# Output projection and attention of the row pairs as one written-out sequence for five queues

## The chip, the core and the metric

The kernel runs on one core of a Trainium2 chip. The metric is the device time of one execution in microseconds. The engines are TensorE (PE, with its weight loads as PEld), VectorE (DVE), ScalarE (ACT), GpSimd (POOL) and SyncE (SP), which here issues all DMAs.

## What is computed

For x of 2048 rows and 1024 columns, all in fp32:

```
xn = layernorm(x)
q, k, v = heads(xn @ wqkv)                  # 32 heads of 32
phi(p)  = concat(softmax(p @ w_phi), softmax(-p @ w_phi))     # per head, 64 features
o       = phi(q) (phi(k)^T v) / (phi(q) (phi(k)^T 1) + 1e-6)
s       = concat_heads(o) @ wo
g       = silu((sigmoid(xn @ w_gate) * (xn @ w_up)) @ w_down)
out     = x + s * g
```

## The kernel before

Every large product is done in the same way. An fp32 operand is split into a high part (an ACT copy that rounds) and a low part (a DVE subtraction), and one product is three matmuls (`mm3`, lines 134 to 136: high by high, high by low, low by high). The 2 by 2 block product is done with seven products of sums of blocks instead of eight, named B11, T2, T3, B21, T1, T4 and B22; the sums are made on POOL.

The stages run one after the other: layernorm with the q, k and v projections, the gated unit (`glu`), the down product with its silu gate g, which goes to DRAM as `g_d`, and last, from 2180 us on, the output projection. Features of q, scaled by their denominators, lie in DRAM as `e_d`.

The output projection takes the rows in eight pairs of 128-row tiles (`NTP` = 8, loop variable `tp_`). For each pair there are two kinds of work:

- **Attention of the next pair** (`attend(tp_ + 1)`, twelve entries). `phi_transpose` turns features with four PE transposes into one of two banks (`tpr`) and splits them with ACT and DVE; the feature tiles are two (`whole(47)` and `whole(48)`, one for each row tile u), each holds one half hb of the heads, and `e_load(u)` refills it when both of its parts q have been turned. `numerator` does eight matmuls of 256 columns into two banks (`nmr`), whose halves are copied (ACT, L684) and added (DVE, L685) into two raw tiles (`oraw`). `o_operands` then makes the seven operands from the raw tiles: one POOL subtraction after the first half (L697), three after the second (L700, L701, L705), in place on the raw tiles, and seven splits.
- **Output of this pair**: seven products with four steps each, 84 matmuls of 512 columns (tiles `x`, `w` or `fa`, `fb` by operand), evacuated by DVE (L1215, L1217, L1224, L1227) and ACT (L1213); for the four finished blocks a multiplication by g and an addition of x on POOL (L1228, L1229; for two blocks of the last pair on DVE), a store (L1230) and `gx_load` (L1191 g, L1192 x), which refills two of four half tiles (`gx`, slots 53 and 54).

In the profile all of `whole(47)` and up are `fc`. The emission of the pair's loop interleaves the two kinds by a count: after each step of a product it takes entries of the next pair's attention while two thirds of the steps are ahead of the entries. A scheduler that works with estimated times then places the instructions on each engine's queue within what the dependencies allow. At the start of the kernel another part is emitted from a list of names (`FIRST`) under `in_order`, which makes each engine's instructions of that part keep the order of emission; `queued` holds the last instruction of each engine.

Of the kernel before, what the change touches and what calls it, by code (L numbers as in the profile page):

```python
# [18 lines left out]
P = 128  # L19
# [14 lines left out]
class Ring:  # L34
# [3 lines left out]
    def next(self):  # L38
        self.n += 1
        return self.items[(self.n - 1) % len(self.items)]  # L40
# [9 lines left out]
def hedgehog_glu_kernel(  # L50
# [65 lines left out]
    def halves(*ids):  # L116
        return [slots[i][:, a] for i in ids for a in range(2)]
# [6 lines left out]
    def pair(i):  # L124
        return slots[i][:, 0], slots[i][:, 1]

    def split(o, src):

        nc.scalar.copy(o[0], src)  # L129
        return nc.vector.tensor_sub(o[1], src, o[0].bitcast(F32))  # L130
# [512 lines left out]
    gx = Ring(halves(54, 53))  # L643
# [7 lines left out]
    def e_load(u):  # L651
        tp_, hb = divmod(e_next[u], 2)
        if tp_ < NTP:
            nc.sync.dma_start(whole(47 + u), e_d[2 * tp_ + u, hb])
        e_next[u] += 1

    def phi_transpose(tp_, u, hb, q):
        ps = tpr.next()
        e = whole(47 + u)
        for j in range(4):  # L660
            k = 4 * q + j
            nc.tensor.transpose(ps[:, j * P:(j + 1) * P], e[:, k * P:(k + 1) * P], ident)  # L662
        if u == 0:
            b = run(phu.next(), 2).rearrange("p a b n -> p (a b n)")
            units_ph[hb, q] = b.rearrange("p (a k t) -> p a k t", a=2, t=256)
        ph, cs = units_ph[hb, q], slice(u * P, (u + 1) * P)
        split((ph[:, 0, :, cs], ph[:, 1, :, cs]), ps.rearrange("p (k t) -> p k t", t=P))
        if q:
            e_load(u)

    def numerator(tp_, hb, q):

        ph = units_ph[hb, q]
        kg = slots[KVB[hb]][:, q].rearrange("p (k m) -> p k m", m=P)
        for b in range(2):
            ps = nmr.next()
            for j in range(2):
                k = 2 * j + b
                for a in range(2):
                    nc.tensor.matmul(ps[:, j * 256:(j + 1) * 256], kg[:, k], ph[:, a, k], start=a == 0, stop=a == 1)  # L680
            hi, lo = [slice(r * 64, r * 64 + 64) for r in (b, 1 - b)]
            o = oraw[hb][hi].rearrange("p u (g t) -> p g u t", t=P)[:, 2 * q:2 * q + 2]
            y, z = [ps[r].rearrange("p (j u t) -> p j u t", j=2, u=2) for r in (hi, lo)]
            nc.scalar.copy(o, z)  # L684
            nc.vector.tensor_add(o, o, y)  # L685
        if q:
            o_operands(tp_, hb)

    def o_operand(tp_, i, b):
        split(pair(of[tp_][i]), b)  # L690

    def o_operands(tp_, hb):
        (b11, b12), (b21, b22) = [(o[:, 0], o[:, 1]) for o in oraw]
        if hb == 0:
            of[tp_] = {i: ofr.next() for i in range(7)}
            o_operand(tp_, B11, b11)
            nc.gpsimd.tensor_sub(b11, b12, b11)  # L697
            return
        o_operand(tp_, B22, b22)
        nc.gpsimd.tensor_sub(b12, b22, b12)  # L700
        nc.gpsimd.tensor_sub(b22, b22, b11)  # L701
        o_operand(tp_, T2, b22)
        o_operand(tp_, T3, b12)
        o_operand(tp_, B21, b21)
        nc.gpsimd.tensor_sub(b21, b21, b22)  # L705
        o_operand(tp_, T1, b11)
        o_operand(tp_, T4, b21)

    def attend(tp_):

        out = []
        for hb in range(2):
            tr = {(u, q): (phi_transpose, tp_, u, hb, q) for u in range(2) for q in range(2)}
            nm = [(numerator, tp_, hb, q) for q in range(2)]

            out += [tr[0, 0], tr[0, 1], tr[1, 0], nm[0], tr[1, 1], nm[1]]
        return out
# [407 lines left out]
    for n, (i, j, cs) in enumerate(dsteps):  # L1125
        w, hs = dready[n]
        for c in cs:
            for u in range(4):
                p = 4 * c + u
                mm3(banks[p], cut(pair(hs[c]), slice(u * P, (u + 1) * P)), pair(w),  # L1130
                    j == 0 and i in (B11, T2, T3, T1), j == NJ - 1, skip_group_check=True)
        wfree.append(w)
        hfree.extend(hs.values())
        if n >= ND - 2 * NJ - 8 and len(WO[B21]) < 4 and hfree:
            WO[B21].append(hfree.popleft())
        if n == 20:
            for hb, s in enumerate(KVB):
                nc.sync.dma_start(slots[s].bitcast(F32).rearrange("p a n -> p (a n)"), kvbd_d[hb])
        while down_prep():
            pass  # L1140
        if j == NJ - 1:
            for c in cs:
                for u in range(4):
                    evacuate(i, 4 * c + u)
        if n and n * 32 // 78 > (n - 1) * 32 // 78 and late:
            t, hb = late.pop(0)
            if t == 0:
                nc.sync.dma_start(zb, zb_d[hb])
            with tc.issue_after(last_split[0]):
                q_task(t, hb)  # L1150
        if 40 <= n < 56 and n % 2 == 0:
            wo_prep(*divmod((n - 40) // 2, 4))
        if n == ND - 2 * NJ:
            assert not late and len(WO[B21]) == 4
            block("x1", 4, 4, F32R)
            for i in (T3, B21):
                side.extend([lambda i=i, k=k: wo_prep(i, k) for k in range(4)])
            side.extend([lambda u=u: e_load(u) for u in range(2)])
        if n == ND - NJ:
            step(1000)  # L1160
            side.extend([lambda fn=fn, a=a: fn(*a) for fn, *a in attend(0)])
# [15 lines left out]

    done = (B21, T1, T4, B22)
    result = [(tp_, i) for tp_ in range(NTP) for i in done]
    gxs = {}  # L1180
# [5 lines left out]
    def gx_load():  # L1186
        if result:
            tp_, i = result.pop(0)
            t, cols = rows(tp_, i)
            g, xt = gxs[tp_, i] = gx.next(), gx.next()  # L1190
            nc.sync.dma_start(g, g_d[t, :, cols])  # L1191
            nc.sync.dma_start(xt, x[t * P:(t + 1) * P, cols])  # L1192

    for _ in range(2):
        gx_load()
    abank = {}
    for tp_ in range(NTP):
        nxt = attend(tp_ + 1) if tp_ + 1 < NTP else []
        n = 0
        u1, u2, y11, y21 = [res.next() for _ in range(4)]  # L1200
        for i in range(7):
            if i in opening:
                abank[i] = amm.next()
            ps = abank[{B21: B11, T4: T3, B22: T1}.get(i, i)]
            o = [h.rearrange("p (k t) -> p k t", t=P) for h in pair(of[tp_][i])]
# [6 lines left out]
            if i == B11:  # L1212
                nc.scalar.copy(u1, ps)  # L1213
            elif i == T2:
                nc.vector.tensor_add(u1, u1, ps)  # L1215
            elif i == T3:
                nc.vector.tensor_add(u2, u1, ps)  # L1217
            else:
                g, xt = gxs.pop((tp_, i))
                t, cols = rows(tp_, i)  # L1220
                eng = nc.vector if tp_ == NTP - 1 and i in (T4, B22) else nc.gpsimd
                if i == B21:
                    y = y11
                    nc.vector.tensor_mul(y, g, ps)  # L1224
                else:
                    y = {T1: u2, T4: y21, B22: u1}[i]
                    nc.vector.tensor_add(y, u2 if i == T1 else u1, ps)  # L1227
                    eng.tensor_mul(y, y, g)  # L1228
                eng.tensor_add(y, y, xt)  # L1229
                nc.sync.dma_start(out[t * P:(t + 1) * P, cols], y)  # L1230
                gx_load()


# [27 lines left out]
```

## Time and profile before

| | |
|---|---|
| median of 3 runs | 2411.07 us (2410.2 to 2412.16) |
| profiled execution | 2411.83 us, span 2410.0 us |
| granted PE clock, mean | 0.997 |
| PE busy, share of the span | 99% |
| DVE, ACT, POOL | 73%, 43%, 40% |
| output projection, first matmul to the end | 2180.51 us to 2410.0 us |

The profile is of one execution; its times are microseconds from the span's start. Matmuls overlap each other, so PE counts as busy even where it only runs at the pace of what feeds it; the distance from one matmul's start to the next tells more. A row of the timeline shows the start, the duration, the engine, the line and the tiles; in brackets stands the idle time before it and what ended it.

### The profile page before, as it was taken

To read this page: it belongs to the slowest core of one execution; us is meant where nothing else is said; L and a number is where in the kernel's file an instruction comes from. 1 tells how busy PE (TensorE), PEld (TensorE's weight loads), DVE (VectorE), ACT (ScalarE), POOL (GpSimd) and SP (SyncE) were. 2 spreads that over 40 slices of the span, in tenths; PEclk is the share of its full clock that TensorE was granted. 3 is DMA by queue.
4 is the path that set the end of the run, shared out by engine and by line. 5 is a ranking of instruction groups with operands and counts; after the bars stand their busy time and mean duration, and the time that the engine had idled before them with its cause. 6 is when DMAs were issued, how large, how long until landed. Compare 5 with 4: busy or idle time off the path is not lost.

```text
span 2410.0 us, 31953 instructions
## 1 busy us (share of the span) xinstructions
PE 2376.2 (99%) x11008; PEld 1974.3 (82%) x11008; DVE 1757.3 (73%) x2323; ACT 1029.4 (43%) x1536; POOL 955.6 (40%) x611
## 2 busy tenths in 40 slices
PE   9999999999999999999999999999999999999998
PEld 8888888888888877888888888888888888878776
DVE  8635777767676688658858888646889988866776
ACT  7334344454544434324434444423443334454443
POOL 1332456656565423122434131323333335414554
PEclk9999999999999999999999999999999999999999
DMA  7688977777676777786877666686666666867554
GB/s 256 243 298 301 367 274 256 271 261 271 250 275 237 260 274 253 247 284 219 280 262 260 210 229 210 210 278 231 218 238 232 225 214 226 283 238 253 183 184 137
DMA packets 232292, 596.31 MB, mean 247 GB/s; under 512 B 30528, under 2 KB 30528, under 8 KB 227520
## 3 DMA queue, kind: packets, MB, share of 16 engines
q1 hardware_dynamic: 232128, 594.25, 70.9%
q8 instruction: 87, 1.43, 0.2%
q14 instruction: 77, 0.63, 0.1%
HBM read 359.01 MB, written 235.14 MB: 247 GB/s over the span
## 4 chain that ended last, share of the span: by engine, by line
PE 83%; DVE 7%; DMA 6%; ACT 2%; issue 2%; POOL 0%; SPq 0%; ACTq 0%; DVEq 0%; POOLq 0%
PE bank L134 27%; PE bank L135 26%; PE bank L136 26%; DVE w L130 2%; PE bank L484 1%; PE bank L283 1%; DMA fc<-qkv_d 1%; PE bank L680 1%; PE bank L662 1%; DMA fc<-xo_d 1%; DMA x<-w_phi 1%; DVE p L130 1%; DVE x L130 1%; ACT w L129 0%; DMA x<-x 0%
## 5 line engine op out<-in xcount | busy, mean ns | idle before, releaser
L134 PE MATMUL bank<-x,w 128*128 128x512 f32 x2352 | 912.1, 390 | 5.9 <-ACT x L129 2.9
L135 PE MATMUL bank<-x,w 128*128 128x512 f32 x2352 | 916.4, 390 | 0.0
L136 PE MATMUL bank<-x,w 128*128 128x512 f32 x2352 | 908.0, 390 | 0.0
L129 ACT CAST w<-fa 128x512 fp32r<-128x512 f32 (+1 forms) x430 | 293.4, 686 | 554.6 <-PE bank L135 367.4
L134 PEld LDWEIGHTS bank<-x,w 128*128 128x128 f32 x2352 | 442.0, 188 | 99.8 <-ACT fb L1039 3.5
L136 PEld LDWEIGHTS bank<-x,w 128*128 128x128 f32 x2352 | 442.1, 188 | 91.9 <-DVE w L130 0.4
L135 PEld LDWEIGHTS bank<-x,w 128*128 128x128 f32 x2352 | 442.2, 188 | 90.1
L130 DVE TENSOR_TENSOR w<-fa,w 128x512 fp32r<-128x512 f32 (+1 forms) x430 | 418.7, 978 | 109.1 <-ACT w L129 101.3
L134 PE MATMUL bank<-w,x 128*128 128x512 f32 x708 | 278.7, 394 | 2.2 <-DVE fc L414 2.2
L136 PE MATMUL bank<-w,x 128*128 128x512 f32 x708 | 277.6, 392 | 2.7 <-DVE x L829 2.7
L135 PE MATMUL bank<-w,x 128*128 128x512 f32 x708 | 276.9, 391 | 0.0
L1049 POOL TENSOR_TENSOR fb<-fb,fc 128x512 f32<-128x512 f32 x57 | 88.1, 1546 | 244.5 <-DVE fc L1048 241.7
L136 PEld LDWEIGHTS bank<-w,x 128*128 128x128 f32 x708 | 133.3, 188 | 32.3 <-DVE x L829 3.8
L134 PEld LDWEIGHTS bank<-w,x 128*128 128x128 f32 x708 | 133.5, 189 | 30.0 <-DVE fc L414 2.5
L135 PEld LDWEIGHTS bank<-w,x 128*128 128x128 f32 x708 | 133.4, 188 | 26.4
L619 POOL TENSOR_TENSOR fc<-fc 128x1024 f32<-128x1024 f32 x32 | 81.5, 2546 | 183.1 <-ACT fc L449 127.5
L1048 DVE TENSOR_TENSOR fc<-fc,bank 128x512 f32<-128x512 f32 x84 | 57.2, 681 | 106.4 <-PE bank L136 98.0
L130 DVE TENSOR_TENSOR x<-fa,x 128x512 fp32r<-128x512 f32 x112 | 112.2, 1002 | 18.7 <-ACT x L129 18.5
L129 ACT CAST w<-fb 128x512 fp32r<-128x512 f32 x112 | 69.3, 619 | 129.1 <-PE bank L135 94.1
L129 ACT CAST p<-fc 128x1024 fp32r<-128x1024 f32 (+2 forms) x97 | 70.8, 735 | 109.8 <-DVE fc L465 63.9
L130 DVE TENSOR_TENSOR p<-fc,p 128x1024 fp32r<-128x1024 f32 (+2 forms) x97 | 105.3, 1094 | 16.0 <-ACT p L129 13.8
L130 DVE TENSOR_TENSOR w<-fb,w 128x512 fp32r<-128x512 f32 x112 | 94.5, 845 | 30.1 <-ACT w L129 25.0
(256 smaller groups left out, 3197.6 us busy)
## 6 DMA issues: line engine op xcount, KB each, us to landing
ws_d<-w SPq DMA_DIRECT2D x112, 512.0 KB, 4.2
w<-ws_d SPq DMA_DIRECT2D x112, 512.0 KB, 4.9
fa<-w_gu SPq DMA_DIRECT2D x84, 512.0 KB, 3.8
fa<-h_d SPq DMA_DIRECT2D x84, 512.0 KB, 4.1
fa<-wf_d SPq DMA_DIRECT2D x32, 1024.0 KB, 7.1
h_d<-fc SPq DMA_DIRECT2D x120, 256.0 KB, 3.3
fc<-e_d SPq DMA_DIRECT2D x48, 512.0 KB, 3.9
fc<-qkv_d SPq DMA_DIRECT2D x80, 256.0 KB, 4.6
```

Of the source, the lines that this page charges most:

```text
L129: nc.scalar.copy(o[0], src)
L130: return nc.vector.tensor_sub(o[1], src, o[0].bitcast(F32))
L134: nc.tensor.matmul(o, a[0], b[0], start=first, stop=False, **kw)
L135: nc.tensor.matmul(o, a[0], b[1], start=False, stop=False, **kw)
L136: nc.tensor.matmul(o, a[1], b[0], start=False, stop=last, **kw)
L283: nc.tensor.matmul(ps[:, gs], r[:, gs], bd[:, 4 * f + g], start=True, stop=True)
L484: nc.tensor.matmul(kvb[g // 2][:, g % 2 * 256:g % 2 * 256 + 256], v[:, g].rearrange("p a f -> p (a f)"), ph[:, g].rearrange("p a f -> p (a ...
L619: nc.gpsimd.tensor_mul(ez, e, zb)
L662: nc.tensor.transpose(ps[:, j * P:(j + 1) * P], e[:, k * P:(k + 1) * P], ident)
L680: nc.tensor.matmul(ps[:, j * 256:(j + 1) * 256], kg[:, k], ph[:, a, k], start=a == 0, stop=a == 1)
L1048: v = nc.vector.tensor_add(b, u2 if q == 3 else u1, bank)
L1049: nc.gpsimd.tensor_mul(g, g, b)
```

## The change

The loop over pairs is replaced by a list of names, `PAIR`, emitted for each of the first seven pairs, and a list `LAST` for the eighth. Everything is emitted under `in_order` for PE, DVE, ACT, POOL and SP, so all five queues keep the order of the list. The functions of attention are cut into single parts: `tr` u hb q (four transposes), `hi` and `lo` (the splits), `nm` hb q b (four matmuls), `cp` and `ad` (their evacuation), `s11`, `sA`, `sB`, `sC` (the POOL subtractions), `x`..`h` and `x`..`l` (the operand splits). `g`..k is one step of a product, `v` its evacuation, `m` and `a` the multiplication by g and the addition of x, `y` the store, `l` the loads of g and x for two results later, `e` u hb a feature load. Attention parts in the list belong to pair `tp_ + 1`. The order of the products within a pair is B11, T2, B21, T3, T1, T4, B22.

For the last pair, the multiplication and addition of block B22 are arranged otherwise: POOL computes u1 * g + x ahead (`rest`), and after the last product DVE multiplies the bank by g and adds the two. The loads of g and x for the last two results go into the feature tiles, which are free by then. `attend` without an argument serves the first pair only, as before; in it a feature load is now emitted ahead of the split of the features that it replaces.

As built, each queue holds the same work as before (on DVE one instruction fewer, on POOL two more), and in the steady pairs the SP queue holds four times (load of g, load of x, store), then four feature loads in a row, where it held feature loads between the others before.

```diff
-    for _ in range(2):
-        gx_load()
-    abank = {}
-    for tp_ in range(NTP):
-        nxt = attend(tp_ + 1) if tp_ + 1 < NTP else []
-        n = 0
...
-            for k in range(4):
-                mm3(ps, (o[0][:, k], o[1][:, k]), pair(WO[i][k]), i in opening and k == 0, k == 3, skip_group_check=True)
-                n += 1
-                while nxt and (13 - len(nxt)) * 3 <= 2 * n:
-                    fn, *a = nxt.pop(0)
-                    fn(*a)
...
-                    nc.vector.tensor_add(y, u2 if i == T1 else u1, ps)
-                    eng.tensor_mul(y, y, g)
-                eng.tensor_add(y, y, xt)
-                nc.sync.dma_start(out[t * P:(t + 1) * P, cols], y)
-                gx_load()
+    def gx_load(n):
+        if n < len(result) and result[n] not in gxs:
+            t, cols = rows(*result[n])
+            late = len(result) - 1 - n
+            g, xt = gxs[result[n]] = halves(47 + late) if late < 2 else [gx[(2 * n + a) % 4] for a in range(2)]
+            nc.sync.dma_start(g, g_d[t, :, cols])
+            nc.sync.dma_start(xt, x[t * P:(t + 1) * P, cols])
...
+    PAIR = """
+        gB110 gB111 gB112 tr100 tr000 hi100 gB113 gT20 vB11 gT21 hi000 gT22 lo100 gT23 lo000 gB210 tr001 tr101 e00
+        hi001 nm000 e10 hi101 lo001 gB211 cp000 lo101 gB212 ad000 nm011 vT2 nm001 cp011 gB213 cp001 ad011 gT30 ad001
+        gT31 gT32 gT33 tr010 vT3 tr111 hi010 nm010 hi111 lo010 gT10 cp010 lo111 tr110 ad010 gT11 e11 hi110 xB11h
+        tr011 lo110 gT12 e01 hi011 xB11l nm101 lo011 s11 gT13 cp101 nm100 ad101 gT40 cp100 vB21 xT1h nm111 ad100
+        aB21 gT41 cp111 vT1 nm110 ad111 gT42 cp110 gT43 ad110 gB220 vT4 sA xB22h lB21 gB221 xB21h xB22l yB21 gB222
+        xT3h xB21l sB gB223 vB22 sC xT2h xT3l xT2l mT1 xT4h xT1l aT1 xT4l mT4 lT1 aT4 yT1 lT4 yT4 mB22 aB22 lB22
+        yB22""".split()
+
+    LAST = ("gB110 gB111 gB112 gB113 vB11 gT20 gT21 gT22 gT23 vT2 gB210 gB211 gB212 gB213 vB21 gT30 gT31 gT32 gT33 aB21 vT3 "
+            "yB21 gT10 gT11 gT12 gT13 vT1 mT1 aT1 gT40 gT41 gT42 gT43 vT4 mT4 aT4 rest yT1 gB220 gB221 gB222 gB223 yT4 vB22 "
+            "aB22 yB22").split()
...
+    def o_sum(which):
+        (b11, b12), (b21, b22) = [(o[:, 0], o[:, 1]) for o in oraw]
+        o, a, b = {"s11": (b11, b12, b11), "sA": (b12, b22, b12), "sB": (b22, b22, b11), "sC": (b21, b21, b22)}[which]
+        nc.gpsimd.tensor_sub(o, a, b)
...
+    def scaled(tp_, i, part):
+        u1, u2, y11, y21 = ys[tp_]
+        g, xt = gxs[tp_, i]
+        y = {B21: y11, T1: u2, T4: y21, B22: u1}[i]
+        last = tp_ == NTP - 1 and i == B22
+        eng = nc.vector if tp_ == NTP - 1 and i in (T4, B22) else nc.gpsimd
+        if part == "m":
+
+            return last or eng.tensor_mul(y, y, g)
+        eng.tensor_add(y, y, y11 if last else xt)
...
+    def last_rest():
+        u1, (g, xt) = ys[NTP - 1][0], gxs[NTP - 1, B22]
+        nc.gpsimd.tensor_mul(u1, u1, g)
+        nc.gpsimd.tensor_add(u1, u1, xt)
...
+    queued.clear()
+    with in_order(*[getattr(mybir.EngineType, e) for e in ("PE", "DVE", "Activation", "Pool", "SP")]):
+        for tp_ in range(NTP):
+            ys[tp_] = [res.next() for _ in range(4)]
+            if tp_ + 1 < NTP:
+                of[tp_ + 1] = {i: ofr.next() for i in range(7)}
+            else:
+                for n in (2, 1):
+                    gx_load(len(result) - n)
+            for name in PAIR if tp_ + 1 < NTP else LAST:
+                ahead, f, found = next((ahead, f, m) for form, ahead, f in pair_forms for m in [re.fullmatch(form, name)] if m)
+                if tp_ + 1 < NTP or not ahead:
+                    f(tp_, *found.groups())
```

More of the change, by code (lines that the diff above doesn't have):

```diff
@@ L642, in hedgehog_glu_kernel @@
     res = Ring(halves(49, 52))
-    gx = Ring(halves(54, 53))
     tpr, nmr, amm = Ring(banks[:2]), Ring(banks[2:4]), Ring(banks[4:])
@@ L655, in e_load, with transposes @@
         e_next[u] += 1
-    def phi_transpose(tp_, u, hb, q):
-        ps = tpr.next()
+    tbank, nbank = {}, {}
+    def transposes(u, hb, q):
+        tbank[u, hb, q] = ps = tpr.next()
         e = whole(47 + u)
@@ L665, in phi_transpose, with phi_part @@
             units_ph[hb, q] = b.rearrange("p (a k t) -> p a k t", a=2, t=256)
+    def phi_part(part, u, hb, q):
         ph, cs = units_ph[hb, q], slice(u * P, (u + 1) * P)
[L667 to L671, printed above, removed]
+        src = tbank[u, hb, q].rearrange("p (k t) -> p k t", t=P)
+        if part == "hi":
+            nc.scalar.copy(ph[:, 0, :, cs], src)
+        else:
+            nc.vector.tensor_sub(ph[:, 1, :, cs], src, ph[:, 0, :, cs].bitcast(F32))
@@ L673, in numerator, with numerators @@
+    def numerators(hb, q, b):
         ph = units_ph[hb, q]
         kg = slots[KVB[hb]][:, q].rearrange("p (k m) -> p k m", m=P)
[L675 to L683, printed above, removed]
+        nbank[hb, q, b] = ps = nmr.next()
+        for j in range(2):
+            k = 2 * j + b
+            for a in range(2):
+                nc.tensor.matmul(ps[:, j * 256:(j + 1) * 256], kg[:, k], ph[:, a, k], start=a == 0, stop=a == 1)
@@ L684, in numerator, with numerators_out @@
+    def numerators_out(part, hb, q, b):
+        hi, lo = [slice(r * 64, r * 64 + 64) for r in (b, 1 - b)]
+        o = oraw[hb][hi].rearrange("p u (g t) -> p g u t", t=P)[:, 2 * q:2 * q + 2]
+        y, z = [nbank[hb, q, b][r].rearrange("p (j u t) -> p j u t", j=2, u=2) for r in (hi, lo)]
+        if part == "cp":
             nc.scalar.copy(o, z)
+        else:
             nc.vector.tensor_add(o, o, y)
[L686 to L690, printed above, removed]
@@ L692, in o_operands @@
-    def o_operands(tp_, hb):
-        (b11, b12), (b21, b22) = [(o[:, 0], o[:, 1]) for o in oraw]
[L694 to L707, printed above, removed]
@@ L709, in attend, with o_part @@
-    def attend(tp_):
+    def o_sum(which):
+        (b11, b12), (b21, b22) = [(o[:, 0], o[:, 1]) for o in oraw]
+        o, a, b = {"s11": (b11, b12, b11), "sA": (b12, b22, b12), "sB": (b22, b22, b11), "sC": (b21, b21, b22)}[which]
+        nc.gpsimd.tensor_sub(o, a, b)
+    def o_part(tp_, i, part):
+        (b11, b12), (b21, b22) = [(o[:, 0], o[:, 1]) for o in oraw]
+        b = {B11: b11, T1: b11, B22: b22, T2: b22, T3: b12, B21: b21, T4: b21}[i]
+        hi, lo = pair(of[tp_][i])
+        if part == "h":
+            nc.scalar.copy(hi, b)
+        else:
+            nc.vector.tensor_sub(lo, b, hi.bitcast(F32))
@@ new lines, in attend, with phi, o_operand, numerator @@
+    def attend():
+        def phi(u, hb, q):
+            transposes(u, hb, q)
+            if q == 1:
+                e_load(u)
+            for part in ("hi", "lo"):
+                phi_part(part, u, hb, q)
+        def o_operand(i):
+            for part in "hl":
+                o_part(0, i, part)
+        def numerator(hb, q):
+            for b in range(2):
+                numerators(hb, q, b)
+                for part in ("cp", "ad"):
+                    numerators_out(part, hb, q, b)
+            if (hb, q) == (0, 1):
+                of[0] = {i: ofr.next() for i in range(7)}
+                o_operand(B11)
+                o_sum("s11")
+            if (hb, q) == (1, 1):
+                for f, a in ((o_operand, B22), (o_sum, "sA"), (o_sum, "sB"), (o_operand, T2), (o_operand, T3),
+                             (o_operand, B21), (o_sum, "sC"), (o_operand, T1), (o_operand, T4)):
+                    f(a)
@@ L711, in attend @@
         out = []
         for hb in range(2):
-            tr = {(u, q): (phi_transpose, tp_, u, hb, q) for u in range(2) for q in range(2)}
-            nm = [(numerator, tp_, hb, q) for q in range(2)]
+            tr = {(u, q): (phi, u, hb, q) for u in range(2) for q in range(2)}
+            nm = [(numerator, hb, q) for q in range(2)]
             out += [tr[0, 0], tr[0, 1], tr[1, 0], nm[0], tr[1, 1], nm[1]]
@@ L1160, in hedgehog_glu_kernel @@
             step(1000)
-            side.extend([lambda fn=fn, a=a: fn(*a) for fn, *a in attend(0)])
+            side.extend([lambda fn=fn, a=a: fn(*a) for fn, *a in attend()])
         if len(dready) == ND:
@@ L1179, in hedgehog_glu_kernel @@
     result = [(tp_, i) for tp_ in range(NTP) for i in done]
-    gxs = {}
+    gx, gxs = halves(54, 53), {}
     def rows(tp_, i):
@@ new lines, in hedgehog_glu_kernel @@
+    for n in range(2):
+        gx_load(n)
+    PAIR = """
[6 more added lines that the diff above has]
+        yB22""".split()
@@ new lines, in hedgehog_glu_kernel, with products @@
+    LAST = ("gB110 gB111 gB112 gB113 vB11 gT20 gT21 gT22 gT23 vT2 gB210 gB211 gB212 gB213 vB21 gT30 gT31 gT32 gT33 aB21 vT3 "
+            "yB21 gT10 gT11 gT12 gT13 vT1 mT1 aT1 gT40 gT41 gT42 gT43 vT4 mT4 aT4 rest yT1 gB220 gB221 gB222 gB223 yT4 vB22 "
+            "aB22 yB22").split()
+    abank, ys = {}, {}
+    def products(tp_, i, k):
+        if k == 0 and i in opening:
+            abank[i] = amm.next()
+        o = [h.rearrange("p (k t) -> p k t", t=P) for h in pair(of[tp_][i])]
+        ps = abank[{B21: B11, T4: T3, B22: T1}.get(i, i)]
+        mm3(ps, (o[0][:, k], o[1][:, k]), pair(WO[i][k]), i in opening and k == 0, k == 3, skip_group_check=True)
@@ new lines, in product_out @@
+    def product_out(tp_, i):
+        ps = abank[{B21: B11, T4: T3, B22: T1}.get(i, i)]
+        u1, u2, y11, y21 = ys[tp_]
+        if i == B11:
+            nc.scalar.copy(u1, ps)
+        elif i == T2:
+            nc.vector.tensor_add(u1, u1, ps)
+        elif i == T3:
+            nc.vector.tensor_add(u2, u1, ps)
+        elif i == B21:
+            nc.vector.tensor_mul(y11, gxs[tp_, i][0], ps)
+        elif i == B22 and tp_ == NTP - 1:
+            nc.vector.tensor_mul(y11, gxs[tp_, i][0], ps)
+        else:
+            o, a = {T1: (u2, u2), T4: (y21, u1), B22: (u1, u1)}[i]
+            nc.vector.tensor_add(o, a, ps)
@@ new lines, in scaled, with store @@
+    def scaled(tp_, i, part):
+        u1, u2, y11, y21 = ys[tp_]
+        g, xt = gxs[tp_, i]
[5 more added lines that the diff above has]
+        eng.tensor_add(y, y, y11 if last else xt)
+    def store(tp_, i):
+        u1, u2, y11, y21 = ys[tp_]
+        t, cols = rows(tp_, i)
+        nc.sync.dma_start(out[t * P:(t + 1) * P, cols], {B21: y11, T1: u2, T4: y21, B22: u1}[i])
```

41 lines of the change are left out of this document (16 added, 25 removed).

## The prediction

> **What bounds the kernel now.** The page first: PE is busy all along and ends last. The output projection therefore costs what its matmuls take plus what they wait for, and the windows view, cut from one first matmul of T1 to the next, gives that per pair.
>
> ```profile
> PE 2376.2 (99%) x11008; PEld 1974.3 (82%) x11008; DVE 1757.3 (73%) x2323; ACT 1029.4 (43%) x1536; POOL 955.6 (40%) x611
> ```
>
> ```profile
> sum 144.46, PE 138.71 PEld 114.29 DVE 102.78 ACT 68.53 POOL 79.43; mean PE 27.74 PEld 22.86 DVE 20.56 ACT 13.71 POOL 15.89
> ```
>
> Five steady pairs take 144.46 us, 28.9 each. No other engine fills a pair (the means: DVE 20.6, POOL 15.9). What PE's own work is shows in the timeline, from start to start:
>
> ```profile
> 2287.20 0.40 PE L134 MATMUL bank<-x,x 128*128 128x512 f32 x1
> ...
> 2289.95 0.60 PE L662 MATMUL bank<-ident,fc 128*128 128x128 f32 x4
> ...
> 2292.61 0.60 PE L662 MATMUL bank<-ident,fc 128*128 128x128 f32 x4
> 2292.97 0.48 PE L134 MATMUL bank<-x,x 128*128 128x512 f32 x1
> 2293.28 0.40 PE L135 MATMUL bank<-x,x 128*128 128x512 f32 x1
> ...
> 2297.18 1.12 PE L680 MATMUL bank<-x,p 128*128 128x256 f32 x8
> 2298.13 0.38 PE L662 MATMUL bank<-ident,fc 128*128 128x128 f32 x2
> ```
>
> Twelve matmuls lie between the first two rows: 2.75 us, 0.229 each, 19.2 for 84. Four transposes take 0.36 and the matmul behind them starts its successor 0.31 instead of 0.23 later: 0.44 a group, 3.5 for eight. Eight matmuls of 256 columns take 0.95: 3.8 for 32. PE's work is 26.6 a pair; the other 2.3 are waits and restarts. In the list of waits for the same stretch PE waits for DVE alone; the longest entry is for the split that frees a transpose bank:
>
> ```profile
> PE bank L662 <- DVE x L130: 2.5, 4, 0.6
> ```
>
> **Part 1: the PE order.** The list puts product steps between the parts of attention, so the chain copy, split, add, split has 0.7 us steps of matmuls to hide under. That can remove up to 2.3 of 28.9 us a pair. It holds if nothing else holds PE's queue, where everything now waits behind a blocked entry.
>
> **Part 2: the SP and POOL orders close a ring.** In the list, e00 and e10 of a pair stand ahead of that pair's own stores but behind yB22 of the pair before. The store waits for aB22, POOL's last addition, and POOL has nine instructions from sA to aB22 in a fixed row: sA sB sC mT1 aT1 mT4 aT4 mB22 aB22. SP waits in order, so the features for tr010 and tr111 can't be asked for before aB22 has ended, though their tiles have been free since tr101. And sA waits for ad110, which waits for nm110, which stands behind tr010 on PE. So the ring: aB22, e00 and e10, tr010 and tr111, PE up to nm110, cp110, ad110, sA to aB22. One turn is one pair, and its length is the pair's time if it is over PE's 26.6. Before, one of two loads was issued between POOL's instructions, and nothing in the list of waits comes from a load in the steady pairs. The rows for its terms:
>
> ```profile
> 2294.04 1.28 POOL L1229 TENSOR_TENSOR fb<-fb,fc 128x512 f32<-128x512 f32 x1
> ...
> 2300.57 1.28 POOL L700 TENSOR_TENSOR fc<-fc 128x512 f32<-128x512 f32 x1 [5.24 <-DVE fc L685]
> 2302.54 1.61 POOL L701 TENSOR_TENSOR fc<-fc 128x512 f32<-128x512 f32 x1 [0.69 <-DVE x L130]
> 2304.23 1.63 POOL L705 TENSOR_TENSOR fc<-fc 128x512 f32<-128x512 f32 x1
> ```
>
> ```profile
> 2295.35 0.34 SPq L1230 DMA_DIRECT2D out<-fb  x1
> 2295.78 0.38 SPq L1192 DMA_DIRECT2D fc<-x  x1
> 2296.22 4.61 SPq L654 DMA_DIRECT2D fc<-e_d  x2
> ```
>
> The landing times of the feature loads (512 KB), and the median of a load of g:
>
> ```profile
> DMA to landing us min/median/max: 3.1/4.2/5.7
> ```
>
> ```profile
> fc<-g_d SPq DMA_DIRECT2D x20, 256.0 KB, 2.9
> ```
>
> ```profile
> 2297.85 0.58 ACT L684 COPY fc<-bank 64x512 f32<-64x512 f32 x1 [2.63 <-PE bank L680]
> ```
>
> ```profile
> 2298.47 0.68 DVE L685 TENSOR_TENSOR fc<-fc,bank 64x512 f32<-64x512 f32 x1 [3.61 <-ACT fc L684]
> ...
> 2301.18 1.22 DVE L130 TENSOR_TENSOR x<-fc,x 128x512 fp32r<-128x512 f32 x1
> ```
>
> - Issue: POOL ends at 2295.32; store, load of x and feature load go out at 2295.35, 2295.78 and 2296.22. The load of x and the store are also ahead of e00 in the list: 0.9.
> - e00 lands after 4.2 (3.1 to 5.7). I take the median: store and load of x are in flight, as at 2296.22, but no feature load just before.
> - e10 is issued 0.43 later; if it queues, 512 KB cost twice the 1.3 between a load of g (2.9) and one of features (4.2), so 0.43 to 2.6 behind e00. I take the middle, 1.5. tr111 waits for it; tr010 lies inside.
> - PE from tr111 to nm110: three groups of transposes 1.3, five halves of numerators 2.4, six product steps 4.1; the last numerator ends 0.16 after its slot; cp110 0.58, ad110 0.68, handovers 0.04 each: 9.4.
> - POOL: L701 starts 1.97 after L700, since the split of the tile that it overwrites must end first; the split itself (2301.18) lasts 1.22 and ends 0.55 behind the POOL instruction, while L1229 on DVE, also from SBUF alone, takes 0.69 beside an idle POOL (part 4). POOL's next one starts 1.69 later, stretched by the next split. DVE still has xB22l, xB21l, xT3l, xT2l, xT1l, xT4l to do, one against each of sA to mT4: 1.97 + 5 x 1.69 = 10.4. The last three go at 1.28 and a handover: 4.0. Sum 14.4; without any collision 12.7.
>
> The ring: 0.9 + 4.2 + 1.5 + 9.4 + 14.4 = 30.4 us. Bounds: 0.9 + 3.1 + 0.43 + 9.4 + 12.7 = 26.5, where PE's 26.6 would rule, and 0.9 + 5.7 + 2.6 + 9.4 + 14.4 = 33.0. So PE waits 30.4 - 26.6 = 3.8 a pair, in place of 2.3: some 1.1 at tr111 (1.5 less the 0.44 of tr010) and 2.5 at tr010.
>
> **Part 3: PE's clock after the wait.** Rows of this kernel's end show what a wait of that size does:
>
> ```profile
> 2387.66 0.80 PE L134 MATMUL bank<-w,fa 128*128 128x512 f32 x1 [2.80 <-ACT fa L129]
> ...
> 2390.69 0.40 PE L136 MATMUL bank<-w,fa 128*128 128x512 f32 x1
> ...
> 2399.03 0.47 PE L134 MATMUL bank<-x,fa 128*128 128x512 f32 x1 [1.60 <-DVE fb L1217]
> ```
>
> After 2.80 us idle, the seven starts up to 2390.69 take 3.03 us instead of 1.6, about half pace, and 1.4 are lost. After 1.60 nothing is: from 2399.03 to the last matmul (part 4) 23 starts take 5.30, 0.23 each. The new wait, 2.5 and soon another 1.1 with four transposes between, lies between the rows, and the slow matmuls would lie on the ring. I count the loss in half of six pairs: 3 x 1.4 = 4.3, with 0 and 8.6 as ends. The Trainium skill ("TensorE: Matmul & The Clock Gate", Part 1: The HAM clock gate) has the clock halved only after an idle window of about 3.4 us; by it nothing would be lost at 2.5, and the sum would be the 3.5 of part 4 alone. The row at 2.80 speaks against so late a point.
>
> **Part 4: the two ends.**
>
> ```profile
> 2180.51 0.47 PE L134 MATMUL bank<-x,fb 128*128 128x512 f32 x1
> ...
> 2378.28 0.39 PE L134 MATMUL bank<-x,x 128*128 128x512 f32 x1
> ...
> 2404.33 0.39 PE L136 MATMUL bank<-x,fb 128*128 128x512 f32 x1
> ```
>
> ```profile
> 2404.76 0.69 DVE L1227 TENSOR_TENSOR fb<-fb,bank 128x512 f32<-128x512 f32 x1 [0.58 <-PE bank L136]
> ...
> 2406.20 0.69 DVE L1229 TENSOR_TENSOR fb<-fb,fc 128x512 f32<-128x512 f32 x1
> ```
>
> These are the first matmuls of pairs 0 and 7, the last matmul, and the first and last of three DVE instructions behind it, 0.72 apart. The span ends 3.80 after 2406.20. First pair: its features were loaded in the stage before, so there is no ring yet, and it holds a whole attention: 26.6. Pairs 1 to 6: 6 x 30.4 = 182.4. Together 209.0 instead of 197.8. Last pair: its operands are ready, no attention lies in it, so 83 x 0.229 = 19.0, then 0.43, two DVE instructions instead of three 0.72, and 3.80: 24.0 instead of 31.7 (which holds the waits of 2.80 and 1.60). Sum: +11.2 - 7.7 = +3.5. The emission of attention for pair 0, the earlier feature load there and the single sums `rest` lie beside other work of PE or POOL: nothing, within 0.5 either way. With the clock +7.8. The profiled execution took 2411.83, so 2419.6; the median lies 0.76 lower: 2419.
>
> **The rivals.** Each time stands for the median; against it, 0.2% is 4.8 us, about what a measurement of this kernel can tell from no change.
>
> - *The clock holds.* The ring as above, no half pace: +3.5, 2414.6. For it: no row between 1.60 and 2.80; transposes break the wait.
> - *Loads land late.* e00 at 5.7, half pace in all six pairs: 6 x (1.5 + 1.4) + 3.5, +21, 2432. For it: two feature loads now leave together, with two more behind.
> - *The ring is short but binds.* Loads land in 3.5, as when alone, POOL misses some collisions: a pair takes 29.8, the sum is even: 2411.
> - *The ring lies inside PE's work* (the other side). The price is one place, POOL's row from sA to aB22: if it ran near 12.7 and the two loads landed together near 3.1, the wait at tr010 is gone, a pair takes 26.6 and some 0.4 of restarts, 27.0. Then 26.6 + 162 + 24.0 = 212.6, -17: 2394. It decides from a pair below 29.0 (6 x 1.4 = 8.4 less than mine with the 3.5 gone). Against it: POOL's own rows above, 1.6 in every pair where DVE splits.
> - *The order isn't kept.* The queues as built follow the list, so this is small: 2411.
>
> **How the numbers follow.** Forecast 0.40, clock holds 0.20, late loads 0.12, short ring 0.12, inside PE 0.13, order not kept 0.03. The predicted time is the first's: 2419, its own range 2412 to 2427. The low end, 2403, lies between the short ring and the fast case and leaves some 0.09 below; the high end, 2430, leaves some 0.1 of the late loads. Faster by over 0.2% (below 2406.2): the fast case and a little of the short ring, 0.15. Within: most of the short ring, the order not kept, over half of the holding clock and the forecast's low edge, 0.27. Slower: 0.58.
>
> **What would show it.** Right: from pair 1 on the first matmuls of pairs lie 30 to 32 apart; PE's transposes are named as waiting for `fc<-e_d`, twice a pair, some 2.5 and 1.1; four feature loads go out in a row right behind the last store; POOL runs from sA to aB22 in about 14.4 with 1.6 to 1.7 under DVE splits; matmuls at 0.43 after tr111 in some pairs; the last pair 24 long. Wrong: feature loads landing before PE gets to tr010, then pairs near 27 and no such wait, or a POOL row under 13.

## The result, and the profile after

The changed kernel takes 2435.4 us (median of 4 runs, 2433.9 to 2436.9) against 2411.0 us of the kernel before on the same chip: a ratio of 1.0100, 95% interval 1.0088 to 1.0112. It is 24 us slower; the forecast was 8. The profiled execution took 2435.58 us, its span is 2433.8 us.

First the page of the changed kernel: the busy times, and the shares of the engines in the chain that ended last:

```profile
PE 2386.5 (98%) x11008; PEld 1982.3 (81%) x11008; DVE 1770.5 (73%) x2322; ACT 1028.6 (42%) x1536; POOL 962.0 (40%) x613
...
PE 79%; DVE 7%; DMA 6%; POOL 4%; issue 2%; ACT 1%; SPq 1%; POOLq 0%; ACTq 0%; DVEq 0%
```

In the same line of the kernel before PE has 83% and POOL 0%; four points of the chain have gone from PE to POOL. The windows view of the changed kernel, cut from the first matmul of one pair to the first of the next, for pairs 1 to 6. The columns are the window, its length, the busy time (and instructions) of PE, PEld, DVE, ACT and POOL, the granted clock, the DMA share and GB/s:

```profile
2207.24:2241.06 33.82, 29.57 (x149) 24.49 (x148) 22.43 (x29) 13.71 (x24) 15.96 (x12) 0.90 0.49 156
2241.06:2275.38 34.32, 29.38 (x150) 24.28 (x148) 22.41 (x29) 13.69 (x24) 15.96 (x12) 0.90 0.49 154
2275.38:2308.78 33.40, 29.97 (x149) 24.80 (x148) 22.51 (x29) 13.69 (x24) 15.95 (x12) 0.90 0.48 158
2308.78:2341.08 32.30, 28.66 (x149) 23.78 (x148) 22.49 (x29) 13.70 (x24) 15.96 (x12) 0.95 0.51 163
2341.08:2374.54 33.46, 28.84 (x149) 23.88 (x148) 22.40 (x29) 13.69 (x24) 15.98 (x12) 0.95 0.50 158
2374.54:2407.57 33.03, 30.20 (x149) 24.90 (x148) 22.47 (x29) 13.70 (x24) 15.96 (x12) 0.90 0.39 128
sum 200.33, PE 176.62 PEld 146.13 DVE 134.71 ACT 82.19 POOL 95.77; mean PE 29.44 PEld 24.36 DVE 22.45 ACT 13.70 POOL 15.96
```

A pair takes 33.4 us, not the 30.4 of the ring's sum nor the 28.9 of before, and no pair has the full clock. The waits of the changed kernel from 2176 us on (in all, times, longest) name what PE waits for; before, PE waited for such a load once there, for 0.6 us:

```profile
PE bank L663 <- DMA fc<-e_d: 21.7, 8, 4.5
...
PE bank L663 <- DVE fb L674: 1.5, 6, 0.3
```

The wait for the split that frees a transpose bank, the longest one of the steady pairs before (2.5), is down to 1.5, as the written order meant it. The wait for the features is new. One turn of the ring in the timeline of the changed kernel (L653 is the feature load, L1217 the load of x, L1278 the store, L663 the transposes, L684 the numerators, L698 POOL's subtractions, L1273 POOL's addition of x):

```profile
2251.68 1.29 POOL L1273 TENSOR_TENSOR fb<-fb,fc 128x512 f32<-128x512 f32 x1
2252.99 0.33 SPq L1217 DMA_DIRECT2D fc<-x  x1
2253.38 0.42 SPq L1278 DMA_DIRECT2D out<-fb  x1
2253.85 1.99 SPq L653 DMA_DIRECT2D fc<-e_d  x2
...
2260.49 1.12 PE L663 MATMUL bank<-ident,fc 128*128 128x128 f32 x4 [4.50 <-DMA fc<-e_d]
2261.79 1.12 PE L663 MATMUL bank<-ident,fc 128*128 128x128 f32 x4 [0.18 <-DMA fc<-e_d]
2262.56 1.20 PE L684 MATMUL bank<-x,p 128*128 128x256 f32 x4
2263.56 0.63 PE L134 MATMUL bank<-w,fa 128*128 128x512 f32 x1
2263.99 0.63 PE L135 MATMUL bank<-w,fa 128*128 128x512 f32 x1
...
2272.91 1.31 POOL L698 TENSOR_TENSOR fc<-fc 128x512 f32<-128x512 f32 x1 [1.54 <-DVE fc L693]
...
2285.99 1.28 POOL L1273 TENSOR_TENSOR fc<-fc 128x512 f32<-128x512 f32 x1
2287.30 0.33 SPq L1217 DMA_DIRECT2D fc<-x  x1
2287.68 0.43 SPq L1278 DMA_DIRECT2D out<-fc  x1
2288.16 0.94 SPq L653 DMA_DIRECT2D fc<-e_d  x2
```

aB22 ends at 2252.97; e00 goes out at 2253.85; tr010 starts at 2260.49, behind 4.50 us of waiting; PE then runs at 0.43 a matmul, half pace; sA starts at 2272.91; aB22 ends at 2287.27, and e00 goes out again 34.31 us after the last time. So the ring is there, in the predicted order and with the predicted members. Over the six turns of this profile its four stretches have these means:

| stretch | predicted | measured |
|---|---|---|
| aB22's end to e00 | 0.9 | 0.88 |
| e00 to tr010 | 4.2 | 5.62 (4.59 to 6.64) |
| tr010 to sA | 10.9, with the clock 11.6 | 12.52 (11.67 to 13.20) |
| sA to aB22's end | 14.4 | 14.37 (14.36 to 14.38) |
| turn | 30.4, with the clock 31.1 | 33.39 |

The end of the changed kernel, from the timeline (L1282 and L1283 are `rest`, L1259 is the last product's evacuation):

```profile
2422.45 0.38 SPq L1278 DMA_DIRECT2D out<-p  x1
...
2426.36 0.69 DVE L1273 TENSOR_TENSOR p<-p,fc 128x512 f32<-128x512 f32 x1
...
2427.32 1.26 POOL L1282 TENSOR_TENSOR fb<-fb,fc 128x512 f32<-128x512 f32 x1 [1.53 <-DMA fc<-g_d]
2428.65 1.26 POOL L1283 TENSOR_TENSOR fb<-fb,fc 128x512 f32<-128x512 f32 x1
2428.71 0.69 DVE L1259 TENSOR_TENSOR p<-fc,bank 128x512 f32<-128x512 f32 x1 [1.65 <-POOL fb L1282]
2429.95 0.69 DVE L1273 TENSOR_TENSOR fb<-fb,p 128x512 f32<-128x512 f32 x1 [0.56 <-POOL fb L1283]
```

Pair 7 takes 26.2 us from 2407.57 to the end instead of the forecast 24.0 (31.7 before): its last matmul starts at 2426.78, 19.2 behind the first, for 19.0 in the forecast, but `rest` still waits for g then, and the last addition waits for `rest`.

### The profile page after: what moved, and what is told of

It reads as the page before. It is cut to its first block, busy times and chain, and to the rows that moved or that the text cites. A ratio compares the mean times of both kernels' runs of the same rounds, so it can differ in the third digit from the quotient of the medians.

```text
span 2433.8 us, 31931 instructions
## 1 busy us (share of the span) xinstructions
PE 2386.5 (98%) x11008; PEld 1982.3 (81%) x11008; DVE 1770.5 (73%) x2322; ACT 1028.6 (42%) x1536; POOL 962.0 (40%) x613
## 4 chain that ended last, share of the span: by engine, by line
PE 79%; DVE 7%; DMA 6%; POOL 4%; issue 2%; ACT 1%; SPq 1%; POOLq 0%; ACTq 0%; DVEq 0%
PE bank L134 25%; PE bank L135 25%; PE bank L136 25%; DVE w L130 2%; DMA fc<-e_d 2%; DMA fc<-xo_d 1%; PE bank L283 1%; PE bank L484 1%; PE bank L684 1%; PE bank L663 1%; POOL fc L698 1%; POOL fc L1272 1%; POOL fc L1273 1%; DMA fa<-wf_d 1%; DVE p L130 1%
## 5 line engine op out<-in xcount | busy, mean ns | idle before, releaser
L130 DVE TENSOR_TENSOR w<-fa,w 128x512 fp32r<-128x512 f32 (+1 forms) x430 | 413.1, 965 | 107.6 <-ACT w L129 100.9
```

## The experiments

**The ring opened.** Only SP's list is changed: three stores (the recorded text counts two, but names three) and two pairs of loads of each pair go behind the next pair's e00 and e10.

```diff
+    LATER = "yT1 lT4 yT4 lB22 yB22".split()
...
             for name in PAIR if tp_ + 1 < NTP else LAST:
+                if tp_ + 1 < NTP and name in LATER:
+                    continue
+                emit(tp_, name)
+                if name == "e10" and tp_:
+                    for name in LATER:
+                        emit(tp_ - 1, name)
```

> The last two stores of each pair and the two pairs of loads of g and x that stand among them (yT1 lT4 yT4 lB22 yB22) are put behind the first two feature loads e00 and e10 of the next pair in SP's list; nothing else moves. Theory (ring over SP's order): the feature loads then wait only for aT1, POOL's fifth instruction from sA (8.7 us after sA starts, not 14.4), so a turn is at most 8.7 + some 1.5 for the loads of g and x that stay ahead + 5.6 landing + 11 to 12.5 to sA = 27 to 28, near PE's own 26.6; pairs 1 to 6 lie 26.6 to 28 apart instead of 33.4, 6 x 5.4 to 6.8 less: 2395 to 2403 us, and PE no longer waits for e_d. Rival (the written PE, DVE and POOL orders are slow of themselves): pairs stay above 30 with another wait in place of the one on e_d, 2415 or more.

Measured: 2396.5 us, ratio to the kernel before 0.9937 (0.9916 to 0.9957). The windows of its pairs 1 to 6, the first and the last of them and the sum:

```profile
2204.65:2231.89 27.24, 26.98 (x149) 22.66 (x148) 22.47 (x29) 13.69 (x24) 15.95 (x12) 1.00 0.57 193
...
2340.78:2367.98 27.20, 26.95 (x149) 22.64 (x148) 22.50 (x29) 13.68 (x24) 15.96 (x12) 1.00 0.45 156
sum 163.33, PE 161.83 PEld 135.91 DVE 134.89 ACT 82.14 POOL 95.75; mean PE 26.97 PEld 22.65 DVE 22.48 ACT 13.69 POOL 15.96
```

PE, DVE, ACT and POOL have the same lists as in the changed kernel and are now done in 27.2 us a pair, at the full clock, with no entry for `fc<-e_d` among the waits. So the written order of the four engines is good, 1.7 us a pair better than the planned one, and the 39 us between these two kernels come from where five names stand in SP's list.

**The ring shortened by two instructions.** The same edit with `LATER = "lB22 yB22"`: e00 then waits for aT4.

> Only lB22 and yB22 are put behind e00 and e10 of the next pair. Theory (one ring, every term one to one): the feature loads wait for aT4 instead of aB22, two POOL instructions or 2.7 us earlier, so pairs 1 to 6 shrink from 33.4 to about 30.7, 16 us in all: 2419, between 2416 and 2423, and PE still waits for e_d by 1 to 2 us a pair. Rival (another loop of the same length holds the pairs): less than 4 us of gain, above 2431.

Measured: 2416.5 us (2413.5 to 2418.7). Its windows:

```profile
2204.19:2233.71 29.52, 27.33 (x150) 22.62 (x148) 22.44 (x29) 13.68 (x24) 15.96 (x12) 1.00 0.54 178
2233.71:2264.92 31.21, 28.94 (x149) 23.93 (x148) 22.49 (x29) 13.69 (x24) 15.95 (x12) 0.95 0.51 169
2264.92:2298.51 33.59, 29.93 (x149) 24.81 (x148) 22.50 (x29) 13.68 (x24) 15.95 (x12) 0.90 0.48 157
...
sum 182.12, PE 168.20 PEld 139.32 DVE 134.71 ACT 82.11 POOL 95.72; mean PE 28.03 PEld 23.22 DVE 22.45 ACT 13.69 POOL 15.95
```

A pair takes 30.4 on the mean, 3.0 less for 2.7 us of POOL work taken out of the ring: the turn is the pair's time. Part of the 3.0 is the clock, whose column tells the pairs apart: four of them have 1.00 and take 29.2 to 29.5, one has 0.95 and takes 31.2, one has 0.90 and takes 33.6.

**The wait filled.** Ten matmuls of 512 columns, whose result tr010 overwrites, ahead of tr010 in every ring, so that PE's idle time is cut into shorter pieces:

```diff
+        for n in range(10 if fill is not None else 0):
+            nc.tensor.matmul(ps, pair(of[fill][T1])[0][:, :P], pair(WO[T1][0])[0], start=True, stop=True)
```

> The order of the changed kernel is kept; ahead of tr010, in pairs 1 to 7's features, ten matmuls of 512 columns into the bank that tr010 then overwrites fill 2.3 us of PE's wait for the feature load, so that PE is idle no longer than about 2 us. Theory (half pace after the wait lies on the ring): the eight transposes and the matmuls behind them run at full pace, 1.4 to 1.6 us a pair in six pairs: 2425 to 2428. Rival (the slow stretch lies beside ACT's and DVE's splits and costs nothing): 2434 to 2437. A third way: what the ten matmuls delay when the load lands early would make it longer than 2437.

Measured: 2433.2 us (2428.4 to 2436.4), a wide spread, with no changed kernel measured beside it. Both were then measured together:

> The changed kernel once more, unaltered, so that the three kernels run beside it can be held against it on one chip: 2435, between 2432 and 2438, if feature loads land as in its first profile (4.6 to 6.6 us, mean 5.6).

> The kernel with ten filling matmuls ahead of tr010 again, now beside the changed kernel. Its first profile had full pace in four of six pairs. Theory (half pace costs up to 1.6 us a pair and lies on the ring): 4 x 1.6 = 6 us, up to 9, below the changed kernel of the same call. Rival (half pace lies beside other work, and the first profile's 7 us came from loads that landed early): within 2 us of it.

Measured: changed kernel 2438.5 us (2436.8 to 2438.9), filled 2431.0 us (2428.0 to 2436.5), 7.5 less. The changed kernel came out 3 us above its first median, with pairs of 33.8 on the mean. The filled kernel's windows in this second run:

```profile
2205.41:2237.01 31.60, 29.64 (x159) 24.54 (x158) 22.41 (x29) 13.68 (x24) 15.99 (x12) 1.00 0.52 166
2237.01:2270.52 33.51, 30.99 (x160) 25.67 (x158) 22.40 (x29) 13.68 (x24) 15.95 (x12) 0.95 0.50 157
...
sum 197.58, PE 183.82 PEld 152.27 DVE 134.71 ACT 82.11 POOL 95.78; mean PE 30.64 PEld 25.38 DVE 22.45 ACT 13.68 POOL 15.96
```

In the filled kernel's two profiles six of twelve pairs have the clock at 1.00; they take 30.8 to 32.3 us, and from tr010 to sA 10.8 to 11.2 where the full pace holds to the end. The other six have 0.95 and take 33.4 to 34.1. In the changed kernel's two profiles no pair of twelve has 1.00. From e00 to tr010 it is 5.8 us on the mean in this second profile and 5.7 in the changed kernel's beside it, so the gain doesn't come from earlier loads. So the half pace lies on the ring and costs about 12.5 - 10.8 = 1.7 us a pair; the filling takes it away in half of the pairs. Why not in all is read below.

**The feature loads cut.** e00 and e10 as four loads of 256 KB, in the order in which PE turns them:

```diff
+        for q in qs or ():
+            c = slice(q * HB, (q + 1) * HB)
+            nc.sync.dma_start(whole(47 + u)[:, c], e_d[2 * tp_ + u, hb][:, c])
```

> The two feature loads at the head of SP's four are cut into halves of 256 KB, in the order in which PE turns them (u0 q0, u1 q1, u1 q0, u0 q1). Theory (a load's landing behind the store, the load of x and the other features goes by the bytes ahead of it and its own): tr010 waits for a first half that lands after some 3.5 us instead of 5.6 and tr111 for the second half 0.5 to 1 later; the pairs shrink by about 2, 12 us in all: 2421 to 2427. Rival (the landing is set by what was queued before, the store and the loads of g and x, or by a fixed time): the first half lands at 5 or later, 2432 or more.

Measured: 2427.8 us (2419.7 to 2432.1). From the first load's issue to tr010 it is now 4.47 us on the mean of six (3.5 to 5.6), against 5.62. Half the bytes save a fifth of the time, so most of the landing isn't set by the load's own bytes. The time and the landing both lie between what the theory and the rival put, and part of the gain is the clock, which has half pace in three rings here instead of six.

**The same wait, with nothing in flight.** The last store of a pair is cut into its first eight rows, which stay ahead of e00 and wait for aB22 there, and the rest, which goes behind e10 with lB22:

```diff
-        yB22""".split()
+        yB22 zB22""".split()
...
+    LATER = "lB22 zB22".split()
...
-        (r"y(\w+)", False, lambda p, i: store(p, i_(i))),
+        (r"y(\w+)", False, lambda p, i: store(p, i_(i), 0, 8 if p + 1 < NTP and i == "B22" else P)),
+        (r"z(\w+)", False, lambda p, i: store(p, i_(i), 8)),
```

> The last store of a pair is cut: its first eight rows (16 KB) stay in front of e00, so that SP still waits for aB22 there; the other 120 rows and the loads lB22 go behind e10. The same wait then, but nearly nothing in flight ahead of e00. Theory (e00 lands late because the store, the load of x and the load of g are being moved ahead of it): e00 is issued 0.45 instead of 0.88 after aB22 and lands in about 4.2 or less instead of 5.6, the ring is 1.8 to 2.4 shorter, 11 to 15 us below the changed kernel of the same call. Rival (the feature loads hold up one another): only the 0.43 goes, 2 to 4 us below it.

Measured: 2418.3 us (2411.7 to 2425.4), 20 below the changed kernel measured beside it, more than the theory's 11 to 15. One of its turns in the timeline:

```profile
2279.64 1.28 POOL L1273 TENSOR_TENSOR fc<-fc 128x512 f32<-128x512 f32 x1
2281.35 0.80 SPq L653 DMA_DIRECT2D fc<-e_d  x2
...
2284.80 0.66 PE L663 MATMUL bank<-ident,fc 128*128 128x128 f32 x4 [0.87 <-DMA fc<-e_d]
2286.32 0.66 PE L663 MATMUL bank<-ident,fc 128*128 128x128 f32 x4 [0.87 <-DMA fc<-e_d]
2286.74 0.91 PE L684 MATMUL bank<-x,p 128*128 128x256 f32 x4
```

From e00 to tr010 it is 3.46 us on the mean of six (3.25 to 3.78) instead of 5.62. So 2.2 us of e00's landing were the store and the loads of x and g put on the queue just before it. Pairs at the full clock take 29.15 to 29.65; from tr010 to sA they need 10.9 to 11.5, and 0.49 + 3.46 + 10.9 + 14.37 = 29.2 is the ring's sum; the gain beyond the theory is the clock, which is at 1.00 in three pairs of six now that the wait is short.

**The end.** The loads for the last two blocks go to the places of e11 and e01 of pair 6, and `rest` ahead of mT4, on top of the opened ring.

```diff
-                for n in (2, 1):
-                    gx_load(len(result) - n)
...
+        if h == "1" and p == NTP - 2:
+            return gx_load(len(result) - 1 - u)
```

> The order with the ring opened (yT1 lT4 yT4 lB22 yB22 behind the next pair's e00 and e10), and in the last pair the loads of g and x for its last two blocks put to the place of e11 and e01 of the pair before, with the single sums (rest) ahead of mT4. Theory (the last pair ended 26.2 us after its first matmul, not 24.0, because these loads went out behind the last store of pair 6): pairs 27.2 apart as with the ring opened, and 2 us less at the end: 2394, 2 below the opened ring alone. Rival (POOL and DVE hold each other up at the end whatever the loads do): 2396, no change against the opened ring.

Measured: 2396.5 us, the same as with the ring opened alone. In its trace 5.8 us lie between the last matmul's start and the end, instead of 6.6 with the opened ring and 7.0 in the changed kernel: less than hoped, and too little for the medians to show. Behind vT1 POOL ran mT1, aT1 and `rest` without a pause, so its row set the end. The next attempt put `rest` ahead of aB21, into a tile thought free:

> On top of the opened ring with the early last loads: rest (u1 * g + x of the last block, two POOL instructions) goes into a free tile, so that it need not wait for vT4, and stands ahead of aB21 in the last pair, where POOL has just finished the pair before. Theory (after the loads were moved, POOL's row mT1 aT1 rest behind vT1 set the end): the last DVE addition follows its own product, some 4.9 us lie between the last matmul's start and the end instead of 5.8 with rest behind vT4, 6.6 with the ring opened alone and 7.0 in the changed kernel; 0.9 less in all, 2395.5, which only the trace can show. Rival (DVE's or SP's own row sets the end): 5.8 stays.

Measured: 2399.9 us, a miss. The timeline says why:

```profile
2386.75 1.29 POOL L1284 TENSOR_TENSOR fc<-fb,fc 128x512 f32<-128x512 f32 x1 [4.51 <-DMA out<-fc]
```

The tile was still being stored: in the opened ring its store goes out only at the start of the last pair. The last product's multiplication by g waited as well, 3.35 us, for the late store of the tile that it writes. With other tiles for both:

```diff
-        u1, z, (g, xt) = ys[NTP - 1][0], ys[NTP - 2][0], gxs[NTP - 1, B22]
+        u1, z, (g, xt) = ys[NTP - 1][0], ys[NTP - 2][2], gxs[NTP - 1, B22]
...
-            nc.vector.tensor_mul(y11, gxs[tp_, i][0], ps)
+            nc.vector.tensor_mul(u1, gxs[tp_, i][0], ps)
```

> rest ahead of aB21 again, but into a tile whose store went out a pair before (block B21's of pair 6), and the last product goes into u1 instead of block B21's tile, so that neither waits for a late store. Theory (POOL's row behind vT1 sets the end of the opened ring): the last DVE addition follows its own product, some 4.9 to 5.1 us lie between the last matmul's start and the end instead of 5.8 with rest behind vT4 and 8.96 in the attempt with the tile in store; about 0.8 below the kernel run beside it, 2395.6. Rival (DVE's or SP's own row sets the end): 5.8 stays.

> The opened ring with the early last loads once more, as the mark for the kernel beside it: 2396, pairs 27.2 apart, 5.8 us from the last matmul's start to the end.

Measured: 2394.0 us, ratio 0.9926 (0.9912 to 0.9939), beside 2394.9 us, 0.9928 (0.9914 to 0.9941). The end of the first in its timeline:

```profile
2386.86 0.39 PE L136 MATMUL bank<-x,fb 128*128 128x512 f32 x1
```

```profile
2387.34 0.69 DVE L1259 TENSOR_TENSOR fb<-fc,bank 128x512 f32<-128x512 f32 x1
2387.35 0.33 SPq L1280 DMA_DIRECT2D out<-p  x1
2388.14 0.69 DVE L1274 TENSOR_TENSOR fc<-fc,fb 128x512 f32<-128x512 f32 x1
```

The evacuation follows the last matmul and the addition the evacuation; the span ends at 2392.0, 5.1 us behind the last matmul's start. POOL's row behind vT1 had been the limit; the two medians differ by less than their intervals. The kernel before took 2413.7 us beside them; these versions beat both kernels.

## Why the prediction was wrong

The direction, the mechanism and most of its terms held; the size was a third of the loss, and the time lies outside the range. Point by point:

- *Part 1, the order of the engines.* Right: the opened ring shows 27.2 us a pair where the rival "inside PE's work" put 27.0. The written order is the better one.
- *Part 2, the ring.* Right in its members and in POOL's row (14.37 for 14.4), in the issue (0.88 for 0.9) and, at the full clock, in the stretch from tr010 to sA (10.8 for 10.9). **The first step that failed is the landing of e00**: the median of the feature loads before, 4.2, was taken, and 5.62 was measured: 6 x 1.4 = 8.5 us. The prediction named the right neighbours, a store and a load of x just ahead, "as at 2296.22", and then took a number that wasn't theirs. That load's own landing, from the loads of its line between 2295 and 2298 us of the kernel before, is

```profile
DMA to landing us min/median/max: 4.9/4.9/4.9
```

Two that left alone, at 2300.5 and 2329.5, landed in 3.2 and 3.1: the median mixes both kinds. Three more left as the one at 2296.22 did, right behind a load of g, a store and a load of x (at 2267.17, 2325.23 and 2354.27), and landed in 5.3, 4.6 and 5.4. The four give 5.05, six tenths of the way from 4.2 to 5.62; what the rest is, no run shows. In the changed kernel the loads of g and x, the store, e00 and e10 all leave within some 4 us. Emptying the queue brought 3.46. The bound of 5.7 from the row of before was nearer the truth than its median.
- *Part 3, the clock.* **The second step that failed is the count**: half pace in three of six pairs, 1.43 each, 4.3 in all. It came in all six and cost 12.52 - 10.9 = 1.6 each, 9.7 in all, 5.4 more than counted. The two steps are one chain: with the later landing the wait at tr010 is 2.5 to 4.5 us instead of 2.5.
- *Part 4, the ends.* Pair 0 took 26.9 for 26.6. The last pair took 26.2 for 24.0: 0.2 are matmuls, and 7.0 instead of 4.95 us lie behind the last matmul's start. "Its operands are ready" and "the single sums lie beside other work" failed: of the 7.0, 0.4 went when the ring was opened, 0.8 with the loads and `rest` ahead of mT4 on top, 0.7 more with `rest` ahead of aB21.
- The sum: 8.5 + 5.4 + 0.3 + 2.2 = 16.4, and the profiled execution lies 2435.6 - 2419.6 = 16.0 above the forecast.

The rival whose number came true is "loads land late": e00 at 5.7, half pace in every pair, a pair of 31.9 + 1.4 = 33.3, 2432 us. It had the pair right to 0.1 and missed only the two ends. It was given 0.12. Its reason didn't hold: in the kernel with nothing in flight e00 and e10 still leave some 0.43 us apart, and e00 is at its reader after 3.46 us. The lateness is that of the store and the loads of g and x ahead, so its 5.7 was the right size for another cause.

The rule weighed at part 3 was read too narrowly. In the timeline of the kernel with nothing in flight half pace follows two waits of 0.87 us with four transposes between: the numerators at 2286.74 last 0.91 instead of 0.72, 3.2 us after the last product's matmul at 2283.54. The Trainium skill ("TensorE: Matmul & The Clock Gate", Part 4: PE-mode transpose) says that a transpose doesn't count as PE-busy in the same way; so read, PE's pause runs from the last product to the first numerators, 4.9 to 7.0 us from start to start in the changed kernel, and the 3.4 us of the rule (Part 1: The HAM clock gate) agree with half pace in every pair. They don't settle a pause as long as the rule's: in another ring of that kernel 3.5 us, from 2220.40 to 2223.93, left the full pace.

There the place of the pause decides as well. Cut fine, the windows view of the changed kernel shows the granted clock (third number from the end) around the pause that the numerators at 2262.56 end:

```profile
2256.70:2258.40 1.70, 0.00 (x0) 0.00 (x0) 0.02 (x1) 0.00 (x0) 0.00 (x0) 1.00 0.89 267
2258.40:2261.81 3.41, 1.13 (x5) 0.74 (x5) 0.00 (x0) 0.11 (x1) 0.00 (x0) 0.50 0.41 161
2261.81:2265.22 3.41, 3.41 (x13) 3.01 (x14) 1.65 (x3) 1.65 (x3) 0.00 (x0) 0.50 0.01 2
2265.22:2266.90 1.68, 1.68 (x13) 1.45 (x12) 0.94 (x3) 1.20 (x3) 0.00 (x0) 1.00 0.21 54
```

Half pace starts while PE is still idle and ends amid its work. In this profile's pairs it starts at 2224.26, 2258.40, 2292.53, 2326.66, 2360.80 and 2391.52 and lasts 3.41 or 6.83 us. These starts lie 10, 10, 10, 10 and 9 times 3.413 us apart, although the turns differ by up to 2 us; so the clock changes at the ticks of a grid that doesn't follow the kernel. In every other profile with half pace in several places it is the same, only the last one being cut off by the kernel's end. Right before each half pace lies a stretch of the grid in which at most five matmuls of products start, where dense work has fifteen. The Trainium skill ("TensorE: Matmul & The Clock Gate", Part 1: The HAM clock gate) calls the window free-running, and these traces agree. So the row at 2.80 in part 3 couldn't give a limit for the length of a wait: there the granted clock is 0.50 from 2387.10 on, before PE resumes at 2387.66. The filled kernel fits too, since its filling lies ahead of the transposes and their waits: from its last filling matmul to the first numerators it is 3.4 to 4.1 us in the six pairs with half pace and 2.5 to 3.9 in the six without. A filling behind the transposes was not tried.

## What to carry to other kernels

When a queue is put in a fixed order, follow each load back to the last instruction that its queue waits for, and add up the turn: a load that stands behind the last store of a stage ties the next stage to the engine that ends this one, and moving five names past two was worth 39 us here. A load's landing is to be taken from the rows with the same neighbours on the queue, not from the median of all; and where a wait of PE grows, its clock belongs in the same sum, since a later landing and a slower PE came together here.

## What had not been expected of the hardware

- A feature load of 512 KB took 3.46 us to reach its reader with almost nothing queued ahead, 5.62 with 768 KB sent in the 2.3 us before it; half of it took 4.47 in the same place.
- Half pace isn't tied to one idle stretch: two of 0.87 us around four transposes were enough in one pair, while in another of the same kernel 0.80 and 1.27 were not.
- The granted clock changes at ticks 3.41 us apart that don't follow the kernel, and half pace lasts one or two of these steps; the same wait of PE can therefore cost 1.7 us in one pair and nothing in the next.
